# Chunked attention with a cosine feed-forward block: new lists of due times and other matmul lengths in the planner

## The chip, the cores and the metric

The kernel runs on one core of one Trainium2 chip. The metric is the device time of one execution in microseconds (us), as the median of a few executions. The engines are PE (TensorE, matmuls), ACT (ScalarE), DVE (VectorE), POOL (GpSimd) and SP (SyncE, which issues the transfers). Each runs its own instructions in their order and waits on semaphores for the others.

## What is computed

```
B, H, S, D = 8, 8, 576, 64                     # q, k, v are float32
scores = q_c @ k_c.T / sqrt(D)                 # within chunks of 64 positions
attn   = exp(scores - max) / (sum + 1e-9)
x      = (attn @ v_c), heads side by side      # 4608 tokens x 512
h      = x @ w_in                              # 512 x 2048
out    = (h * cos(h)) @ w_out                  # 2048 x 512
```

The weights come as 64-bit floats, and the result has to be near to the 32-bit one.

## The kernel before, in words

The 4608 tokens are worked on in nine tiles of 512 (`TOK`), t = 0 to 8. A matmul of full precision is made of three: each operand is split into a high part (a cast to fp32r) and a low part (the rest), and high x high, high x low and low x high are added up in PSUM. So a product of 128 rows by 512 columns is three matmuls, and the step "hidden" of one block of 128 features is twelve.

First stage (tiles 0 and 1, and the attention of tile 2). Weights are loaded and decoded: two ACT operations and one on DVE (`split_weight`, lines 564 to 571) give a 32-bit weight, then a high and a low part (`copy_by`, lines 503 and 505; `two_by`, line 509). PE takes turns: twelve matmuls of `hidden` (x by w_in, into one of two banks `h`), then twelve of `project` (g by w_out, into four banks `acc`) for the block three back. Between them ACT and DVE make g = h cos(h) by four steps (`activated`, lines 886 to 889: ACT, DVE, ACT, DVE), and then the parts `g_hi` (ACT or DVE) and `g_lo` (DVE or POOL). The last DVE step of the four (line 889) frees the bank of h for the hidden product two blocks later. Attention of the tiles 0 to 2 (scores in 64x64 matmuls) is fitted in between. POOL, DVE and ACT also make sums of weight blocks (`whole_again`, `sums_of_w`, `high_parts`, `low_parts`), which `keep_sums` stores (line 988).

At the end of this stage come the differences of tile 2 (`halves`, lines 1094 and 1104). They are written to the tiles `pts` and `vt`, which also hold tile 1's results on their way out (`finish`; stores at line 958).

From tile 2 on, hidden products are made by seven products in place of eight on halves of the features and of x (Strassen's scheme as Winograd gives it): `single_pair` for tile 2 and `wide_pair` for two tiles at once (3 and 4, 5 and 6, 7 and 8). Their weights are streamed back from memory (`combo`). The scores and weighted sums of the next tiles come between them.

The order of work is made when the program is built. Each step is entered by `piece(engine, length, run, *after, lag, other, main)`; `other` is a second engine that may do it. `in_order` hands all pieces of a stage to `placed`, a model of five engines: it takes the engine that can begin soonest, and of its pieces that can begin within 0.2 us of that the one with the lowest due time, and notes the start. Then the pieces are written into the program by their starts. A step with two engines goes to the one that took it. The due times come from four lists, one for each stage: `DUE_FIRST` (648 pieces), `DUE_SECOND` (1062, tile 2 and tiles 3 and 4), `DUE_NEXT` (596, tiles 5 and 6) and `DUE_LAST` (463, tiles 7 and 8). The search that found lists (`trials`) is switched off here; it minimised the end and the mean start of the matmuls marked `main`.

What the model holds: a length for each piece, a lag to whoever waits, a charge for POOL and DVE at work together (`PORT`), a change of ACT's tables (`TABLE`), a slower PE after a pause, and, in the first stage alone, a delay of PE's instructions. A step on SP is booked with 0.1 to 1.8 us, a store of a result with 0.1 us and 2.5 us more until it has landed (line 1462). The order of the loads of inputs and weights (`FIRST_LOADS`) is fixed, and they are not moved by the lists.

From the second stage on, all PE work is one chain, so the lists leave its order alone:

```
    def pe(length, run, *after):
        stream[0] = piece(PE, length, run, stream[0], *after, main=True)
        return stream[0]
```

In the first stage, `hidden` and `project` are such a chain, and the attention's PE steps can move against it.

Of the kernel before, what the change touches and what calls it, by code (L numbers as in the profile page):

```python
# [159 lines left out]
)  # L160


DUE_SECOND = (
# [296 lines left out]
def attention_then_cos_ffn(ctx: ExitStack, tc, qT, kT, v, w_in, w_out, out, wide):  # L460
# [759 lines left out]
    def made_by(key, run, *args):  # L1220

        def go():
            made[key] = run(*args)
        return go
# [11 lines left out]
    split = {}  # L1236
# [882 lines left out]
```

## Time and profile before

| | us |
|---|---|
| median of 3 runs (lowest to highest) | 792.94 (792.94 to 793.42) |
| the profiled execution | 792.41 |
| its span, first to last instruction | 790.4 |
| PE busy | 772.8 (98%) |
| DVE busy | 579.6 (73%) |
| ACT busy | 473.4 (60%) |
| POOL busy | 302.8 (38%) |

Matmuls overlap: the profile shows each of them with an end that lies past the start of the next one, so a group is best measured from start to start. A wait stands in square brackets behind the instruction that waited, with the idle time of its engine and what ended it. "issue" stands where the profile shows nothing that was waited for. SPq are the queue instructions by which SP starts transfers.

### The profile page before, as it was taken

The page shows a single profiled execution, that of the slowest core. Times are in us where ns is not written, and L with a number is a line of the kernel's source. Part 1 is how long each engine was busy: PE and PEld are TensorE (multiplying, and loading weights), DVE is VectorE, ACT ScalarE, POOL GpSimd, SP SyncE. Part 2 cuts the span into 40 slices and gives each one's busy share as a digit, 9 for nine tenths or more (in the row PEclk, how much of TensorE's full clock was granted, in tenths as well). Part 3 has the DMA queues.
Part 4 walks back from the last instruction along what each step waited for, and adds up shares of the span by engine and source line. Part 5 has one row for each costly group of instructions (what it writes and reads, how often), then busy time and mean ns, then how long its engine had stood idle before and what let it go on. Part 6 is the DMA issues. An engine that isn't in the chain of part 4 may idle for free.

```text
span 790.4 us, 15213 instructions
## 1 busy us (share of the span) xinstructions
PE 772.8 (98%) x5818; PEld 673.7 (85%) x5818; DVE 579.6 (73%) x913; ACT 473.4 (60%) x872; POOL 302.8 (38%) x240
## 2 busy tenths in 40 slices
PE   7999999999989999999999999999999999999997
PEld 6878888887879988888888888888888888888886
DVE  6988898987887898885786968886896664554421
ACT  6999975454866566645664456454763464555522
POOL 3454476556734382211134842221265621221100
PEclk9999999999999999999999999999999999999999
DMA  9992707566975755845646358647553265543431
GB/s 341 412 417 110 241 15 258 182 232 213 321 250 181 221 191 189 296 164 188 222 141 216 113 181 300 191 149 239 171 203 104 78 214 181 189 164 107 158 109 54
DMA packets 72744, 156.19 MB, mean 198 GB/s; under 512 B 7776, under 2 KB 22624, under 8 KB 72672
## 3 DMA queue, kind: packets, MB, share of 16 engines
q1 hardware_dynamic: 72672, 155.22, 57.6%
q8 instruction: 46, 0.75, 0.4%
q14 instruction: 26, 0.21, 0.1%
HBM read 117.44 MB, written 37.75 MB: 196 GB/s over the span
## 4 chain that ended last, share of the span: by engine, by line
PE 85%; ACT 6%; DMA 4%; DVE 3%; issue 1%; POOL 0%; SPq 0%; ACTq 0%; DVEq 0%; POOLq 0%
PE acc L494 44%; PE h L494 32%; PE a L494 9%; DMA w_in<-in_w_in_dram 2%; DMA qt<-in_qT_dram 1%; ACT half L571 1%; ACT w L569 1%; ACT g L888 0%; ACT g L886 0%; DMA out_dram<-pts 0%; ACT g_hi L505 0%; PE a L1321 0%; ACT e L678 0%; DVE pts L509 0%; DMA out_dram<-vt 0%
## 5 line engine op out<-in xcount | busy, mean ns | idle before, releaser
L494 PE MATMUL acc<-w_out,g_hi 128*128 128x512 f32 x1124 | 336.3, 381 | 0.6 <-ACT pts L505 0.6
L494 PEld LDWEIGHTS acc<-w_out,g_hi 128*128 128x128 f32 x1124 | 210.1, 190 | 30.4 <-ACT pts L505 1.0
L509 POOL TENSOR_TENSOR g_lo<-g,g_hi 128x512 fp32r<-128x512 f32 x78 | 109.8, 1410 | 282.7 <-ACT g_hi L505 178.0
L494 PE MATMUL acc<-w_out,g_lo 128*128 128x512 f32 x562 | 213.1, 379 | 0.0
L494 PE MATMUL h<-x,w_in 128*128 128x512 f32 (+1 forms) x864 | 199.0, 357 | 2.9 <-DVE g L889 2.4
L494 PEld LDWEIGHTS h<-x,w_in 128*128 128x128 f32 x864 | 150.0, 190 | 23.9 <-DVE g L889 3.4
L494 PE MATMUL h<-w_in,w_in 128*128 128x512 f32 (+1 forms) x576 | 136.2, 354 | 0.8 <-DVE w_in L1139 0.7
L494 PEld LDWEIGHTS acc<-w_out,g_lo 128*128 128x128 f32 x562 | 106.5, 190 | 15.1
L494 PEld LDWEIGHTS h<-w_in,w_in 128*128 128x128 f32 x576 | 99.2, 190 | 14.4 <-DVE w_in L1139 2.2
L505 ACT CAST g_hi<-g 128x512 fp32r<-128x512 f32 x98 | 60.3, 618 | 44.7 <-PE acc L494 29.2
L1145 DVE SCALAR_TENSOR_TENSOR g<-g,h 128x512 f32<-128x512 int32 (+1 forms) x40 | 23.0, 576 | 73.7 <-ACT g L1142 73.4
L494 PE MATMUL a<-x,w_in 128*128 128x512 f32 x288 | 70.2, 380 | 0.0
L494 PEld LDWEIGHTS a<-x,w_in 128*128 128x128 f32 x288 | 54.2, 189 | 8.2 <-ACT a L1136 0.7
L509 DVE TENSOR_TENSOR g_lo<-g,g_hi 128x512 fp32r<-128x512 f32 x38 | 35.2, 931 | 26.1 <-ACT g_hi L505 24.6
L1136 ACT COPY h<-h 128x512 f32<-128x512 f32 (+1 forms) x40 | 19.4, 485 | 55.4 <-PE h L494 42.7
L1149 ACT ACTIVATE g<-g 128x512 f32<-128x512 f32 (+1 forms) x72 | 41.9, 582 | 17.1 <-DVE g L1145 16.8
L1149 ACT ACTIVATE w_in<-w_in 128x512 f32<-128x512 f32 x48 | 29.8, 628 | 10.1 <-DVE w_in L1145 10.1
L509 POOL TENSOR_TENSOR e<-e,z 128x512 f32<-128x512 f32 x14 | 17.9, 1290 | 43.4 <-DVE z L763 35.6
L505 ACT CAST g_hi<-w_in 128x512 fp32r<-128x512 f32 x24 | 14.9, 620 | 29.2 <-PE acc L494 26.4
L1142 ACT ACTIVATE g<-h 128x512 int32<-128x512 f32 (+1 forms) x40 | 20.5, 511 | 18.2 <-PE h L494 17.3
L1145 DVE SCALAR_TENSOR_TENSOR w_in<-w_in,w_in 128x512 f32<-128x512 int32 x24 | 28.6, 1190 | 2.4 <-ACT w_in L1142 1.2
L888 ACT ACTIVATE g<-g 128x512 f32<-128x512 f32 x32 | 20.2, 631 | 14.6 <-DVE g L887 14.5
(205 smaller groups left out, 1182.4 us busy)
## 6 DMA issues: line engine op xcount, KB each, us to landing
w_in<-combo SPq DMA_DIRECT2D x112, 512.0 KB, 4.0
combo<-w_in SPq DMA_DIRECT2D x56, 256.0 KB, 3.3
gathered<-w_in SPq DMA_DIRECT2D x48, 256.0 KB, 3.5
qt<-in_qT_dram SPq DMA_DIRECT2D x36, 256.0 KB, 4.8
kt<-in_kT_dram SPq DMA_DIRECT2D x36, 256.0 KB, 5.2
w_in<-in_w_in_dram SPq DMA_DIRECT2D x16, 512.0 KB, 9.4
w_out<-in_w_out_dram SPq DMA_DIRECT2D x16, 512.0 KB, 9.6
w_in<-gathered SPq DMA_DIRECT2D x24, 256.0 KB, 3.0
```

Of the source, the lines that this page charges most:

```text
L494: kept(nc.tensor.matmul(*args, **kw))
L505: kept(nc.scalar.copy(out=out, in_=in_))
L509: kept(eng.tensor_tensor(out, a, b, op=op))
L569: lambda: kept(nc.scalar.activation(w(), upper.bitcast(F32), AF.Prelu, scale=2.0 ** -(MORE // 8), alpha=-(2.0**32))),
L571: lambda: kept(nc.scalar.activation(low, lower, AF.Copy, scale=LOWEST)),
L888: lambda: kept(nc.scalar.activation(g, g, AF.Sin, bias=0.5 * math.pi)),
L1136: kept(nc.scalar.copy(out=out, in_=in_))
L1142: kept(nc.scalar.activation(g.bitcast(I32), h, AF.Identity, bias=0.25, scale=0.5 / math.pi))
L1145: kept(nc.vector.scalar_tensor_tensor(g, g.bitcast(I32), -2.0 * math.pi, h, op0=ALU.mult, op1=ALU.add))
L1149: kept(nc.scalar.activation(g, g, AF.Sin, bias=0.5 * math.pi))
```

## The change

Three of the four lists get other numbers, as many as before: `DUE_FIRST`, `DUE_SECOND` and `DUE_NEXT`. `DUE_LAST` stands in the diff as context and is not changed. The correlation of ranks between old and new list is 0.65, 0.76 and 0.69, so the order is another one throughout. The lengths of PE pieces in the planner become shorter: 0.68 to 0.648 for three matmuls of 512 columns, 2.72 to 2.592 for twelve, 0.35 to 0.336, 0.706 to 0.672 and 1.362 to 1.296. No operation is added, removed or changed; what moves is the order on ACT, DVE, POOL and SP, the engine of steps that have two, and in the first stage the place of the attention's PE steps. The first lines of each list:

```diff
 DUE_FIRST = (
-    19.07, 9.7, 18.15, 19.93, 20.46, 14.17, -7.36, 18.95, 59.8, 25.74, 17.73, 33.29, 23.7, 22.9, 47.19, 12.37,
-    19.85, 0.82, 97.2, -15.62, 1.32, 2.6, 14.1, 35.52, 24.56, 26.31, -1.59, 49.53, 35.88, 33.69, -25.45, 38.61,
...
+    8.4, 47.45, -291.79, -58.6, 42.54, 115.52, 3.71, 510.8, 41.47, 33.14, -55.91, 16.87, 25.16, 147.1, -147.69,
+    16.63, 26.11, 22.2, 162.21, -18.7, 29.26, 38.45, -29.26, -4.08, 7.83, 49.32, 81.95, 10.5, 34.24, 24.93, 14.19,
...
 )
 DUE_SECOND = (
-    5.26, 2.29, 11.01, 13.29, 4.38, 3.21, 5.68, 16.46, -34.46, 25.06, 22.89, 86.91, 25.49, 121.17, 37.24, 22.92,
-    25.11, 17.31, 18.05, 45.53, -55.15, -43.44, -15.1, -40.72, -3.76, -60.06, 31.92, 7.1, 11.2, -34.2, -20,
...
+    -12.85, 2.21, 2.31, 3.75, 7.22, 3.78, 4.82, 4.73, 34.21, 4.92, 3.46, 22.89, 82.26, 18.21, 88.69, 755.07,
+    -15.61, 20.48, 21.88, 57.79, 81.17, 0.65, 2.14, 4.32, 2.53, 3.32, 4.25, 39.9, 6.37, 17.38, 107.92, 9.35,
...
 )
 DUE_NEXT = (
-    -39.57, -31.5, -27.38, -30.94, -35.82, -3.65, -25, -26.04, -8.41, -21.66, 15.69, -26.96, -20.56, -17.77,
-    -17.41, 21.43, 12.15, -12.73, 13.68, 12.16, 8.18, 16.96, -8.11, 20.22, -21.39, -14.9, 17.41, -5.99, -14.23,
...
+    20.68, 0.95, -10.86, 1.45, -3.38, -1.44, -17.55, 24.42, 3.81, -5.59, -57.9, 96.14, 11.4, 22.2, -19.2, 78.23,
+    2.02, -57.15, -68.3, 96.01, -8.58, -2.59, 48.9, 6.14, -34.28, -7.27, -5.72, 12.26, 11.5, 12.86, -5.77, 15.17,
...
 )@@ the planner's lengths @@
-                    PE, 0.68, go, stream if cc else None, split["in", fc], bank_at, *x_done[t][2 * cc : 2 * cc + 2],
+                    PE, 0.648, go, stream if cc else None, split["in", fc], bank_at, *x_done[t][2 * cc : 2 * cc + 2],
...
-                PE, 2.72, made_by(key, hidden, t, fc), stream, split["in", fc], bank_at, *before,
+                PE, 2.592, made_by(key, hidden, t, fc), stream, split["in", fc], bank_at, *before,
...
-                PE, 2.72, made_by(key, project, u), stream, given[u], split["out", fu], *free, *before, pairs=12, main=True
+                PE, 2.592, made_by(key, project, u), stream, given[u], split["out", fu], *free, *before, pairs=12, main=True
...
-            0.68 if half is None else 0.35, lambda: out_part(t, fc, sub, half), low_of.get((t, fc)),
+            0.648 if half is None else 0.336, lambda: out_part(t, fc, sub, half), low_of.get((t, fc)),
...
-            return product_piece(7 * k + j, 0.706, go, *deps)
+            return product_piece(7 * k + j, 0.672, go, *deps)
...
-            return product_piece(n0 + j, 1.362, go, *deps, *(x_lows.get((t, j), ()) if k == 0 else ()))
+            return product_piece(n0 + j, 1.296, go, *deps, *(x_lows.get((t, j), ()) if k == 0 else ()))
```

## Rows read from the trace of the kernel before

**Rows 1.** The span cut into stretches (start:end in us), then its length, the busy us and instruction count of each engine, PE's granted clock, the busy share of the transfer engines and GB/s.

```profile
core 0: us, PE busy (x) PEld busy (x) DVE busy (x) ACT busy (x) POOL busy (x), PEclk, DMA share, GB/s
0.00:20.00 20.00, 14.66 (x294) 12.32 (x296) 12.56 (x23) 12.52 (x37) 6.47 (x11) 1.00 0.92 342
20.00:60.00 40.00, 38.86 (x348) 32.40 (x349) 35.80 (x63) 39.58 (x62) 19.75 (x15) 1.00 1.03 414
60.00:100.00 40.00, 39.44 (x241) 34.04 (x240) 35.71 (x50) 38.98 (x63) 19.07 (x15) 1.00 0.47 166
100.00:180.00 80.00, 80.00 (x605) 69.31 (x604) 70.31 (x115) 48.51 (x90) 50.71 (x50) 1.00 0.52 179
180.00:200.00 20.00, 18.21 (x177) 15.55 (x179) 14.03 (x18) 9.74 (x19) 13.73 (x14) 1.00 0.60 207
200.00:220.00 20.00, 18.95 (x163) 16.74 (x154) 16.89 (x38) 17.49 (x58) 13.17 (x15) 1.00 0.88 304
220.00:240.00 20.00, 18.00 (x220) 15.97 (x219) 15.06 (x33) 10.97 (x29) 6.58 (x5) 0.91 0.71 236
240.00:280.00 40.00, 40.00 (x495) 36.62 (x494) 33.16 (x78) 26.23 (x74) 14.62 (x13) 1.00 0.65 206
280.00:300.00 20.00, 19.70 (x110) 17.21 (x110) 18.95 (x21) 12.10 (x25) 17.89 (x11) 1.00 0.62 200
300.00:460.00 160.00, 160.00 (x1213) 139.53 (x1212) 128.36 (x195) 88.74 (x147) 56.39 (x39) 1.00 0.57 186
460.00:620.00 160.00, 159.97 (x1212) 139.53 (x1212) 123.96 (x190) 88.42 (x144) 56.26 (x39) 1.00 0.58 191
620.00:790.40 170.40, 165.05 (x771) 144.53 (x769) 74.84 (x100) 80.16 (x135) 28.20 (x20) 1.00 0.43 142
```

**Rows 2.** The waits of PE over the span: the tile it was to write, what released it, then us in total, times and the longest.

```profile
PE h L494 <- DVE g L889: 2.4, 3, 1.8
PE a L494 <- issue: 2.0, 1, 2.0
...
PE h L494 <- DVE w_in L1139: 0.7, 2, 0.5
```

**Rows 3.** PE in order of time around its stalls: start, us until the shown end of the last of the group, what, and the idle time before it with its releaser.

```profile
38.02 0.48 PE L494 MATMUL h<-x,w_in 128*128 128x512 f32 x1 [0.27 <-DVE g L889]
...
49.88 0.48 PE L494 MATMUL h<-x,w_in 128*128 128x512 f32 x1 [0.34 <-DVE g L889]
...
56.98 0.66 PE L777 MATMUL a<-ident,e 128*128 128x128 f32 x4 [0.30 <-DVE x L851]
...
83.61 0.70 PE L494 MATMUL acc<-w_out,g_hi 128*128 128x512 f32 x2 [0.56 <-ACT pts L505]
...
184.05 0.59 PE L494 MATMUL acc<-w_out,g_hi 128*128 128x512 f32 x2
184.48 0.38 PE L494 MATMUL acc<-w_out,g_lo 128*128 128x512 f32 x1
186.65 0.70 PE L494 MATMUL h<-x,w_in 128*128 128x512 f32 x2 [1.79 <-DVE g L889]
...
208.62 0.94 PE L494 MATMUL h<-w_in,w_in 128*128 128x256 f32 x6 [0.53 <-DVE w_in L1139]
...
210.69 0.49 PE L494 MATMUL h<-x,w_in 128*128 128x256 f32 x2 [0.48 <-DVE g L1152]
...
233.42 0.26 PE L494 MATMUL a<-kt,qt 64*64 64x64 f32 x1 [2.00 <-issue]
...
289.49 0.71 PE L494 MATMUL h<-w_in,w_in 128*128 128x256 f32 x4 [0.22 <-DVE w_in L1139]
```

**Rows 4.** One step of the chain that ended last, where PE is full: start, us, what.

```profile
117.55 2.59 PE h L494 x12
```

**Rows 5.** One stretch right after the wait by "issue", with the columns of the first group.

```profile
233.40:236.80 3.40, 3.38 (x13) 2.71 (x13) 2.84 (x6) 1.29 (x8) 0.00 (x0) 0.50 0.50 169
```

**Rows 6.** The same chain ahead of the stall at 184 us.

```profile
174.18 2.39 DMA out_dram<-vt
...
176.69 0.12 DVE vt L1094
...
179.38 3.38 DMA out_dram<-pts
...
182.84 0.88 DVE pts L1094
...
185.99 0.61 DVE g L889
```

**Rows 7.** SP in order of time at the same place: start, us that the group took to issue, what and how many.

```profile
171.22 2.18 SPq L988 DMA_DIRECT2D combo<-w_in  x4
...
178.75 1.23 SPq L958 DMA_DIRECT2D out_dram<-pts  x2
...
181.12 2.83 SPq L988 DMA_DIRECT2D combo<-w_in  x4
```

**Rows 8.** A subtraction on DVE at two places, and the one on POOL beside the second, in order of time on their engines.

```profile
168.81 0.69 DVE L509 TENSOR_TENSOR g_lo<-g,g_hi 128x512 fp32r<-128x512 f32 x1
...
78.98 1.66 DVE L509 TENSOR_TENSOR w_in<-w,w_in 128x512 fp32r<-128x512 f32 x1
...
78.65 1.45 POOL L509 TENSOR_TENSOR g_lo<-g,g_hi 128x512 fp32r<-128x512 f32 x1
```

307 rows, old and new, of tables (DUE_FIRST, DUE_NEXT, DUE_SECOND) are left out of this document.

## Prediction

> **What bounds the kernel now.** I read the stretches first: for each part of the span the table gives busy time by engine, and the reader is to look at how far TensorE (PE) falls short of the stretch's length [rows 1]. In the first 20 us it lacks 5.34 us, while inputs arrive. After that it lacks 1.14 + 0.56 us up to 100 us, nothing to 180, 1.79 in 180 to 200, 1.05 in 200 to 220, 2.00 in 220 to 240, nothing to 280, 0.30 to 300, and then 0.03 us in the whole 320 us that follow. The last stretch lacks 5.35 us, which is the end of the program after its last matmul. So the kernel is bound by PE, and PE is full from 300 us on. The second view, PE's waits, names who releases it: the cosine product of VectorE (DVE) that frees a bank of `h` (2.4 us in three waits), a 2.0 us wait for which nothing visible is the cause ("issue"), and a sum on DVE (0.7) [rows 2]. The third, PE in order of time, gives each stall its place [rows 3]: 38.02, 49.88, 56.98, 83.61, 186.65, 208.62, 210.69, 233.42 and 289.49 us, nine in all that matter.
>
> Idle time understates a stall, since a matmul's shown end lies past the next one's start. At 184.48 us the next start is 2.17 us away, where twelve matmuls in 2.59 us [rows 4] give 0.216 each: 1.95 us lost. The two matmuls after it take 0.70 us, where such a pair takes 0.59 in the same rows [rows 3]: 0.11 more. That is 2.06 us for 1.79 of idle, so I add 0.27 us for each stall. One stall has a sequel: after 2.00 us of idle at 231 us, the granted clock is 0.50, the lower of the two levels, for 3.40 us [rows 5], which is 1.70 us of work. The 1.79 us of idle at 185 us had no such sequel: the clock of that stretch is 1.00 [rows 1].
>
> What a perfect order could give back after 20 us is therefore 6.87 (idle) + 9 x 0.27 = 2.43 + 1.70 = 11.0 us. No order of the other engines does better without a gain in the loading stage, whose loads are asked for in a fixed list that stays as it is.
>
> **The change, part by part.** The lengths (0.68 to 0.648 for three matmuls, 2.72 to 2.592 for twelve) are only numbers in the planner; no matmul gets shorter. By themselves they are worth 0 us. They do bring the planner to what the chip does: 2.592 is the 2.59 us of the chain [rows 4]. The old plan thought PE 5% slower than it is, so what it called just in time came late on the chip where the other engines had no slack. That is a reason why a search with the new lengths can see stalls that the old one could not, and it holds where engines beside PE are nearly full.
>
> The three new lists rank ACT, DVE, POOL and SP work anew, and let some pieces change engine. No work is added, so I cost each stall group:
>
> (a) 20 to 100 us, 1.70 us idle + 4 stalls x 0.27 = 2.8 us. Here ScalarE (ACT) is busy 78.56 of 80 us: it, not PE, is the tightest. DVE has 8.5 us free and POOL (GpSimd) 41 us [rows 1]. High parts and bank copies may go to DVE, low parts to POOL, so an order that unloads ACT by a few of its 0.6 us casts exists. I take 1.7 us back. Bounds: all 2.8, or 1.0 lost if one stall of the size of 83.61 (0.56 + 0.27) is added.
>
> (b) 184 us, 2.06 us. The chain of waits here is not one of engine load [rows 6]: DVE stands at the differences of the third token tile (line 1094), whose target tiles are still being read by two output stores, landing 2.39 and 3.38 us after their start, and the cosine product that frees PE's bank is queued on DVE behind them. The second of these stores began at 179.38 because SP, in order, had issued other transfers first: 2.18 us for four stores of weight sums, then stores and loads [rows 7]. The planner books 0.1 us of SP for such a step and 2.5 us to landing, and the new code keeps both numbers. So the search does not see the cause; it can help only by moving the differences or the cosine product. I take 0.6 us back, less than a third. Bounds: all 2.06, or the loss of rival 3.
>
> (c) 200 to 220 and 280 to 300 us, 1.35 us idle + 3 x 0.27 = 2.2 us. These wait for a sum and a cosine product of single pairs [rows 2, 3], chains of short steps between PE products whose order is fixed by the program. I take 0.6 back; bounds 2.2, or 0.5 lost (one such stall more).
>
> (d) 231 us, 2.00 + 0.27 + 1.70 = 4.0 us. PE stands in the middle of 128 short score matmuls and waits for nothing that the profile shows. I take it for the delivery of its own instructions (that nothing else shows is my only ground), and PE's order in this stage is a chain fixed by the program, with the same count before it. The second list does not steer it. I take 0 back; bounds 0 and 4.0, the latter if the number of waits inserted ahead of it shifts the point.
>
> (e) After 300 us, 0.03 us idle. Two lists (the second's later half and the third) reorder stages which cannot get better. I take 0.3 us lost, one small stall; bounds 0 and 1.6 (two stalls like 208.62, 0.53 + 0.27 each).
>
> Sum: -1.7 - 0.6 - 0.6 - 0 + 0.3 = -2.6 us. The profiled execution took 792.41 us (span 790.4 and 2.0 around it), so 789.8 on its terms; the runs shown have a median 0.53 us higher, so 792.94 - 2.6 = **790.3 us**.
>
> **Where a page speaks against it.** A subtraction on DVE (`g_lo` and the weights' low parts, line 509) took 0.69 us at 168.81 us with POOL idle, and 1.66 us at 78.98 us, while POOL ran one of the same kind from 78.65 on [rows 8]. So work sent to POOL in stretch (a) is not free: at up to 0.97 us each, nine more pieces on POOL use up DVE's 8.5 us, and then nothing of (a) comes back. The Trainium skill (GPSIMD Engine Reference, 1. Specifications) says that GpSimd's interfaces to SBUF are shared with VectorE and contend with VectorE instructions that have two SBUF inputs; both operations are of that kind, and the trace agrees. By that rule taken alone the sum would be -2.6 + 1.7 = -0.9 us. The planner has a term for this, so I leave (a) as it is and give the case to rival 2.
>
> **Rivals.** 1. The stall at 231 us goes too, or shrinks to nothing: -2.6 - 4.0 gives 786.3 us. For it: its place hangs on a count of instructions, and waits are inserted anew by the new order. Against it: the matmuls ahead of it are the same in number. 13%.
>
> 2. The order changes and the time does not. The stalls at 184 and 231 us, 6.1 of the 11.0 us, have causes that the planner does not hold (SP's issue time, instruction delivery), and (a) is held back by POOL's contention; what comes back is lost in (e). Time 792.9 us, within 1.6 either way. 26%.
>
> 3. Slower: the wait on the output stores grows. At 181.12 us SP issues four more stores of weight sums, 2.83 us [rows 7]. If the new order makes these sums ready before the last output stores, SP issues them first, the store that DVE waits for lands 2.83 us later, and PE's idle of 1.79 becomes 4.6. It decides from 2.00 us of idle on, where the clock fell at 231 us: then 1.70 us come on top. +2.83 + 1.70, the 0.6 of (b) not gained, the rest as forecast (-1.7 - 0.6 + 0.3): +2.5, so 795.4 us. For it: neither SP's time nor the order of its issues is in the plan. Against it: the sums wait for POOL, which was busy 13.73 of 20 us there. 18%.
>
> **How the numbers follow.** The forecast has 43%, rival 1 13%, rival 2 26%, rival 3 18%. A change of under 0.2% (1.6 us) can't be told from none. Faster is forecast and rival 1, 0.56; same 0.26; slower 0.18. The likeliest case's own range is 787.5 to 791.3: from half of what it could still gain in (a) to (c), to the edge of what can be told. The range of all goes from 785.0, where (a) to (c) come back whole (7.1 us) and a little of (d), to 795.4, rival 3.
>
> **What would show it right or wrong.** Right: the stalls at 38 to 84 us mostly gone, with ACT's busy share in 20 to 100 us a little lower; a stall near 180 us still released by a DVE product behind line 1094 and an output store; a stall of about 2 us by "issue" among the score matmuls with half the clock after it; and 0.3 us or less of idle after 300 us. Wrong: the early stalls unchanged, a clock that fell at a second place, or new idle after 300 us. If the loading stage's 5.34 us of idle shrinks, I missed a source of gain, since I hold it bound by loads that stay as they are.

## The result: 0.6% slower, and the profile after

The changed kernel took 797.13 us (median of 6, 796.36 to 797.84), the kernel before on the same chip 792.94 (median of 6, 791.88 to 795.56): a ratio of 1.006 with a 95% interval of 1.0045 to 1.0076. The forecast was 790.3 us with a range up to 795.4, so the time lies outside it, on the other side. The profiled execution of the changed kernel took 796.36 us (span 794.6), 4.0 us more than that of before (792.41, span 790.4).

All line numbers of the changed kernel are higher by one: its line 495 is the matmul of line 494, 890 the product of 889, 1095 the difference of 1094. First its span in stretches, with the columns of [rows 1]:

```profile
0.00:20.00 20.00, 15.11 (x260) 12.91 (x260) 11.21 (x23) 11.26 (x34) 5.73 (x10) 1.00 0.93 343
20.00:60.00 40.00, 38.33 (x376) 32.26 (x377) 36.28 (x63) 38.77 (x62) 22.47 (x18) 1.00 1.03 414
60.00:100.00 40.00, 40.00 (x245) 34.85 (x244) 34.09 (x48) 38.67 (x61) 23.59 (x18) 1.00 0.48 166
100.00:180.00 80.00, 78.14 (x594) 67.32 (x593) 66.47 (x102) 47.39 (x85) 49.10 (x51) 1.00 0.49 171
180.00:200.00 20.00, 17.55 (x81) 14.74 (x80) 17.57 (x22) 10.66 (x22) 13.71 (x11) 1.00 0.60 193
200.00:220.00 20.00, 18.92 (x239) 16.71 (x238) 16.68 (x32) 16.55 (x53) 13.85 (x15) 1.00 0.92 310
220.00:240.00 20.00, 19.28 (x239) 17.27 (x238) 17.64 (x40) 15.19 (x41) 7.11 (x7) 1.00 0.82 267
280.00:300.00 20.00, 18.94 (x108) 16.88 (x108) 17.65 (x19) 12.52 (x25) 16.91 (x11) 1.00 0.61 188
300.00:460.00 160.00, 159.34 (x1208) 138.56 (x1207) 122.99 (x194) 89.17 (x147) 56.98 (x39) 1.00 0.57 188
460.00:620.00 160.00, 158.30 (x1201) 137.09 (x1200) 122.13 (x191) 86.81 (x143) 49.56 (x35) 1.00 0.58 191
```

Compare PE's busy time with the length of each stretch, and with [rows 1]. PE was full from 100 to 180 us and short by 0.03 us from 300 to 620; now it lacks 1.86 us in the first, and 0.66 + 1.70 = 2.36 us in the second. Past 20 us, two stretches are better. 60 to 100 us is full (0.56 us short before), but 20 to 60 us lost as much (1.67 for 1.14). 220 to 240 us is 0.72 us short (2.00 before), and the granted clock is 1.00 where it was 0.91.

The new stalls, PE in order of time as in [rows 3]:

```profile
128.86 1.16 PE L495 MATMUL a<-kt,qt 64*64 64x64 f32 x64 [1.50 <-issue]
183.52 0.70 PE L495 MATMUL h<-x,w_in 128*128 128x512 f32 x2 [1.51 <-DVE g L890]
189.90 1.35 PE L495 MATMUL h<-x,w_in 128*128 128x512 f32 x5 [0.93 <-DVE g L890]
495.64 1.56 PE L495 MATMUL h<-w_in,w_in 128*128 128x512 f32 x6 [0.62 <-ACT h L1137]
585.10 0.48 PE L495 MATMUL acc<-w_out,g_lo 128*128 128x512 f32 x1 [0.98 <-POOL g_lo L510]
```

I measured every stall over 0.3 us in both traces from matmul start to matmul start, as the forecast did for the one at 184 us, and added them up by stretch. Left out is a gap of 0.40 us at 20.02 us in the kernel before, the end of the loading. The stall at 231 us has its 1.70 us of half clock [rows 5] with it:

| us | before | after | difference |
|---|---|---|---|
| 20 to 100 | 2.13 | 2.07 | -0.06 |
| 100 to 180 | 0 | 2.19 | +2.19 |
| 180 to 200 | 1.95 | 2.78 | +0.83 |
| 200 to 230, without the next | 1.33 | 2.45 | +1.12 |
| stall at 231, with half clock | 3.90 | 0 | -3.90 |
| 280 to 300 | 0.38 | 1.22 | +0.84 |
| 300 to 460 | 0 | 1.18 | +1.18 |
| 460 to 620 | 0 | 2.19 | +2.19 |
| sum | 9.69 | 14.08 | +4.39 |

The span grew by 4.2 us. Against the sum stand 0.45 us less idle in the first 20 us (4.89 after, 5.34 before) and the 0.40 us at 20.02 us; 0.7 us I can't place. So the lists cost about 8.3 us in stalls, and 3.9 us came back at a place where the forecast expected nothing.

Three views name what the new stalls wait for. DVE and SP around 182 us (start, us, what; idle before it and its releaser):

```profile
182.17 0.69 DVE L1095 TENSOR_TENSOR pts<-e 128x512 f32<-128x512 f32 x1 [6.52 <-DMA out_dram<-pts]
182.78 0.68 DVE L890 TENSOR_TENSOR g<-h,g 128x512 f32<-128x512 f32 x1
```

```profile
174.85 2.20 SPq L989 DMA_DIRECT2D combo<-w_in  x4
177.14 1.97 SPq L959 DMA_DIRECT2D out_dram<-pts  x3
```

DVE stands 6.52 us at the difference that overwrites `pts`, and the product that frees PE's bank is queued behind it. The store that it waits for left SP after four stores of weight sums, which took 2.20 us. In the wide stages it is ACT that stands. Its waits for these transfers over the span, in the changed kernel; the kernel before had one of 1.0 us and one of 2.8 us:

```profile
ACT w_in L1143 <- DMA gathered<-w_in: 11.5, 5, 3.8
ACT g_hi L506 <- DMA w_in<-gathered: 6.6, 3, 2.7
```

The last of them, ACT and SP in order of time:

```profile
580.76 0.63 ACT L1143 ACTIVATE w_in<-w_in 128x512 int32<-128x512 f32 x1 [3.76 <-DMA gathered<-w_in]
...
582.75 1.27 ACT L506 CAST g_hi<-g 128x512 fp32r<-128x512 f32 x2
```

```profile
572.99 2.91 SPq L492 DMA_DIRECT2D w_in<-combo  x2
576.01 0.37 SPq L1757 DMA_DIRECT2D gathered<-w_in  x1
```

ACT may not overwrite `w_in` before its store to `gathered` has left it. That store stood on SP behind two loads. ACT's casts of `g_hi` came after it, then POOL's `g_lo`, for which PE waited 0.98 us.

### The profile page after: what moved, and what is told of

It is laid out like the page before. It is cut to its first block, busy times and chain, and to the rows that moved or that the text cites. A ratio compares the mean times of both kernels' runs of the same rounds, so it can differ in the third digit from the quotient of the medians.

```text
span 794.6 us, 15217 instructions
## 1 busy us (share of the span) xinstructions
PE 773.1 (97%) x5818; PEld 673.4 (85%) x5818; DVE 573.5 (72%) x908; ACT 474.2 (60%) x874; POOL 307.5 (39%) x243
## 4 chain that ended last, share of the span: by engine, by line
PE 82%; ACT 5%; DVE 4%; DMA 4%; issue 2%; SPq 1%; POOL 1%; ACTq 0%; DVEq 0%; POOLq 0%
PE acc L495 42%; PE h L495 31%; PE a L495 9%; DMA w_in<-in_w_in_dram 2%; DMA kt<-in_kT_dram 1%; ACT w L570 1%; ACT half L572 1%; SPq L492 1%; DMA gathered<-w_in 1%; DVE w L565 1%; DMA out_dram<-pts 1%; ACT g L889 0%; ACT L889 0%; ACT g L887 0%; DVE g L888 0%
## 5 line engine op out<-in xcount | busy, mean ns | idle before, releaser
L510 POOL TENSOR_TENSOR g_lo<-g,g_hi 128x512 fp32r<-128x512 f32 x75 | 107.9, 1440 | 271.7 <-ACT g_hi L506 124.3
L1140 DVE TENSOR_TENSOR w_in<-h,w_in 128x512 f32<-128x512 f32 (+1 forms) x40 | 22.6, 582 | 15.4 <-PE h L495 10.6
L1153 DVE TENSOR_TENSOR g<-w_in,g 128x512 f32<-128x512 f32 x32 | 28.5, 892 | 3.7 <-ACT g L1150 2.8
L565 DVE SCALAR_TENSOR_TENSOR w<-w,half 128x512 uint32<-128x512 uint32 x32 | 27.6, 866 | 3.9 <-ACT w L570 2.7
```

The lines of the kernel that those rows point to most:

```text
L510: kept(eng.tensor_tensor(out, a, b, op=op))
L565: kept(nc.vector.scalar_tensor_tensor(bits, bits, 3, low, op0=ALU.logical_shift_left, op1=ALU.bitwise_or))
L1140: kept(nc.vector.tensor_tensor(out, a, b, op=ALU.add))
L1153: kept(nc.vector.tensor_tensor(g, h, g, op=ALU.mult))
```

## Experiments

**One list at a time.** Both sets of lists and lengths stand in one program, and a flag for each of the four stages chooses the set; each stage keeps exactly the order that its parent has there (the state that the planner hands from stage to stage is set to the parent's). The edit, shown at two of its places:

```diff
+NEW = (1, 0, 0, 0)
...
-                PE, 2.592, made_by(key, hidden, t, fc), stream, split["in", fc], bank_at, *before,
+                PE, 2.592 if NEW[0] else 2.72, made_by(key, hidden, t, fc), stream, split["in", fc], bank_at, *before,
...
-        close(ends, DUE_SECOND if u == 1 else DUE_NEXT)
+        close(ends, ((OLD_SECOND, DUE_SECOND) if u == 1 else (OLD_NEXT, DUE_NEXT))[NEW[now[0]]])
```

First stage alone, flags (1, 0, 0, 0):

> First stage planned with the new list and new lengths, the three later stages in the order of the kernel before. From the starts of the same score matmuls in the two traces (198.50 against 201.75 us) the first stage lost 3.25 us. Theory (each list brings its own stalls, and the stall at 231 us is a delivery of instructions held up behind loads that the second list places): the first stage's loss comes alone and the stall near 233 us with its half clock is there again, so 792.9 + 3.2 = 796.2 us. Rival (the stall at 231 us hangs on the count of PE instructions in the first stage): it is gone here, so 796.2 - 4.2 = 792.0.

791.15 us, ratio 0.9975 (0.9961 to 0.9990). Four stalls of the changed kernel's first stage are there, each within 0.3 us (0.98 at 53 us, 1.66 at 126, 1.40 at 181, 1.10 at 188). The first score matmul after 229 us starts 2.4 us later than before, at 231.73. And the stall at 231 us with its half clock is gone. So the first list costs 2.4 us and takes away a stall that belongs to the second stage; the time is near the rival's 792.0 us and far from the theory's 796.2.

Second stage alone, (0, 1, 0, 0):

> Second stage alone by the new list and lengths. Between the same matmuls the second stage gained 1.4 us net: 4.2 for the stall at 231 us with its half clock, less 2.8 of new stalls. Theory: 792.9 - 1.4 = 791.5 us, no half clock. Rival (count of instructions in the first stage): the stall stays, 792.9 + 2.8 = 795.7 us.

791.87 us, ratio 0.997 (0.9957 to 0.9983). The stall at 231 us is 0.33 us. The second list's own are there: 0.65, 0.88, 1.21, 0.40, 0.37 and 0.45 us at 215, 222, 290, 311, 368 and 388 us. The time is the theory's; but as the first list alone takes the stall at 231 us away too, neither list is its one cause.

Third alone, (0, 0, 1, 0):

> Third list (tiles 5 and 6) alone, with its lengths. The starts of the same matmuls say +2.3 us for this stage, which was free of stalls before. Theory: 792.9 + 2.3 = 795.2 us, with stalls of some 0.8 and 1.4 us near 493 and 580 us, each behind an ACT step that waits for a store of the kept g. Rival (the stage loses only because the stage ahead of it left other work over): 792.9 us, no stall after 460 us.

794.83 us, ratio 1.0014 (0.9999 to 1.0029). It loses 1.96 us at 493 us, and 0.47 and 1.14 us at 583. The stall at 231 us (2.54 us) and its half clock stay.

Fourth alone, (0, 0, 0, 1), where the list is the old one and only lengths differ:

> Last stage alone, whose list is the same and whose lengths in the planner are the new ones. The traces show no stall there in either kernel. Theory: 792.9 us within 0.5. Rival (the shorter lengths themselves take away slack that the chip needs): 0.5 us or more above.

792.25 us, ratio 0.998 (0.9967 to 0.9993), with no new stall after 235 us (the 0.38 us at 290 us is that of the kernel before). The new lengths do no harm there. Why the time is 1.0 us below the kernel before the trace doesn't say.

All but the third, (1, 1, 0, 1):

> The changed kernel with the old list and old lengths in the stage of the tiles 5 and 6 alone. Theory (each stage's loss is its own): the stalls at 493 to 584 us go, 2.3 us: 794.8 us. Rival (a stage's loss is made up or passed on by the next): within 1 us of the changed kernel's 797.1.

793.27 us, ratio 1.0001 (0.9991 to 1.0012), 3.9 us under the changed kernel's median where 2.3 were expected. Its PE is full from 460 to 620 us, so the third list's loss is its own and nothing makes it up later. The theory stands, its size was low: this stage has 2.19 us of stalls in the profile, and the third list alone cost 1.6 us, so not all of the 3.9 us is explained. Nor do the first and the second list add up: each alone was 1.4 to 2.1 us under the kernel before, since each takes away the same stall at 231 us, and together (with the last stage's lengths) they gain nothing.

The new lengths with all the old lists:

> The new lengths with the old lists. A due time is only a rank within the run of the planner's model. Theory (lists and lengths belong together: with other lengths the same ranks give another order with more stalls): over 800 us. Rival (ranks carry over): 793 us within 2.

One execution: 822.25 us, with PE short in every stretch (153.73 of 160 us busy in 300 to 460). These lists belong to the lengths they came with; the last stage's list did not suffer from the new ones (run e4).

**Who issues the stores.** Tile 1's results leave through `pts` and `vt`. In the first of these runs they leave by other tiles (`w` and `half`), on top of the extra matmuls of run e5 further down:

```diff
-        if t == 1 or not whole:
+        if not whole:
```

> The same as the run before, and tile 1's results leave through the tiles of the weight sums (w, half) in place of vt and pts, so that the differences of tile 2 on DVE share no tile with an output store. Theory (the 2.06 us stall at 184 us is DVE's wait for those stores): it goes, 788.7 - 2.0 = 786.7 us. Rival (the cosine product would come late anyway, or the sums on POOL now wait for the stores and hold the start of the second stage): 788.7 us or more.

799.26 us, ratio 1.0079 (1.0052 to 1.0106). The theory fell as I had put it. DVE in order of time:

```profile
188.55 0.69 DVE L509 TENSOR_TENSOR w<-w_in 128x512 f32<-128x512 f32 x1 [8.33 <-DMA out_dram<-w]
```

Another room moves the wait to whoever uses that room next, here the weight sums. DVE waits 8.33 us for a store that SP issued only at 183.31 us; in the kernel before it had waited 3.05 us for the store of `pts`. What stays is the rival: the store leaves late. So the next edits leave the tiles alone and let POOL issue the stores: the products h cos(h) that a wide stage sets aside for the second of its two tiles (`gathered`) in the kernel of run e3, tile 1's results in the changed kernel and in the kernel before, and both in the changed kernel.

```diff
-                kept(nc.sync.dma_start(out=gathered[fc], in_=v[g]))
+                kept(nc.gpsimd.dma_start(out=gathered[fc], in_=v[g]))
...
-            nc.sync.dma_start(out=to, in_=os[b::2])
+            (nc.gpsimd if t == 1 else nc.sync).dma_start(out=to, in_=os[b::2])
```

> The third list alone, as before, but with the stores of the kept g issued by POOL instead of SP (in all three wide stages), so that they do not stand behind loads on SP. Theory (the new stalls of this stage, 1.96 us at 493 and 1.6 us at 583, come from ACT waiting for such a store that SP issued late): both go, and the run is 2.5 us or more below that with the third list alone, at some 792.3 us. Rival (ACT and POOL are late there by their own work): the stalls stay, 794.8 us or more, POOL's issuing added.

793.37 us, ratio 1.0002 (0.9982 to 1.0022): the stalls at 493 and 583 us are gone (0.31 us at 587 stays). So the third list's stalls are the wait for SP. The time agrees, but less sharply: 0.7 us above the kernel before in place of 1.6, with intervals that overlap.

> The changed kernel with tile 1's results alone issued by GpSimd in place of SP. Theory: DVE's wait of 6.52 us for the store of `pts` falls to under 3, the stall at 181.6 us (1.68) goes: 795.4 us; the stalls at 494.6 and 583 us stay. Rival (the store's own 4.22 us bounds it, whoever issues it): 797.

795.08 us, ratio to the kernel before 1.0033 (1.0018 to 1.0047). DVE's wait for the store is 3.27 us in place of 6.52 (the store lands 2.07 us earlier, and DVE comes to it 1.18 us later), the stall at 182 us is gone, and the rest is untouched:

```profile
180.10 0.70 DVE L1095 TENSOR_TENSOR pts<-e 128x512 f32<-128x512 f32 x1 [3.27 <-DMA out_dram<-pts]
```

> The changed kernel with two kinds of stores issued by GpSimd in place of SP: tile 1's results (the store in `finish`) and the rounded weights of the wide stages (`gathered`). Order otherwise as changed. Theory (SP issues in order, so a store that is ready waits behind others; the planner books SP 0.1 us): the stall at 181.6 us (1.68) goes or falls under 0.5, those at 494.6 (0.78) and 583 (1.41) go, about 3.5 us together: 793.6 us. Rival (the stores are late by the transfer itself, or GpSimd issues them later than SP would because it works in order too): 797 or more.

792.90 us, ratio 0.9995 (0.9976 to 1.0014): 4.2 us under the changed kernel, with no stall left at 182 or 494 us and 0.22 us at 592. ACT's wait of 3.76 us at 581 us is now:

```profile
579.34 0.63 ACT L1143 ACTIVATE w_in<-w_in 128x512 int32<-128x512 f32 x1 [1.73 <-DMA gathered<-w_in]
```

Two edits on who issues the stores give back all that the change had lost, without touching a list.

> The kernel before with tile 1's results issued by GpSimd in place of SP. Theory: the second store of `pts` starts when its copy is made and not at 179.38 us, the stall at 184.5 us (2.06 us) goes: 2 us faster, 790.7 us, the stall at 231 us with its half clock unchanged. Rival: GpSimd is 13.7 of 20 us busy there and issues late, or the transfer bounds it: 792.7 us, within 1.

790.42 us, ratio 0.997 (0.9957 to 0.9983). The stall at 184 us fell from 1.95 to 1.21 us, not to nothing:

```profile
186.86 2.86 PE L494 MATMUL h<-x,w_in 128*128 128x512 f32 x12 [1.05 <-DVE g L889]
```

The one at 231 us stayed (2.00), but in the profiled execution no half clock followed. So the time is as the theory had it, but by another sum: 0.74 us of that stall and, in this execution, 1.70 of half clock. Over all runs the second part is an estimate: a mean granted clock of 0.9986 against 0.9972 for the kernel before beside it is worth 0.0014 x 790 = 1.1 us.

**What the stall at 231 us is.** The queue that brings instructions, in a short stretch: packets, MB and share. Of the kernel before from 230.8 to 231.2 us, just before PE stands:

```profile
q8 instruction: 1, 0.02, 14.7%
```

Of the changed kernel from 231.4 to 231.6 us, 2 us before its score matmuls, which start at 233.43 us:

```profile
q8 instruction: 1, 0.02, 27.5%
```

Each kernel has 46 such packets in all (0.75 MB, so 16 KB each). In the kernel before, the first of the 128 score matmuls starts at 229.31 us and the packet is fetched 1.56 us later; PE runs out of instructions and goes on at 233.42 us, 1.61 us after this packet has ended. In the changed kernel it comes before the score matmuls. The Trainium skill (Runtime: NRT & Kernel Launch, The ~15µs preamble/postamble breakdown) says that instructions are fetched ahead without an instruction asking for it; the trace agrees, as nothing issues these packets. That one fetched late stalls PE is shown by the runs here.

Counting PE's own instructions (matmuls, weight loads, semaphores) in the traces makes the place plain. In all 19 traces, the n-th packet, from 0, never begins before PE has begun 256n + 152 of them (874 packets). In all nine traces that have the stall at 231 us, PE stops with 4033 begun, whatever the order of the other engines. So the packet after number 3736 (n = 14) has the time of 297 instructions, many of them short, to come. In the kernel before it began 5.7 us after that number and was too late; in the changed kernel it began 2.3 us after it. What delays a packet is not settled. In the traces the median delay is 0.9 us where other transfers moved under 50 GB/s in the following us, and 3.2 us where they moved over 330; no run changed that alone.

To move the fetches I put 24 products of 64x64 (48 matmuls and as many weight loads in the trace, where the expectation counts 48 instructions) into an idle run of PE at 10.4 us of the plan:

```diff
+        for _ in range(small):
+            matmul(b[:CH, :CH], ident[:CH, :CH], ident[:CH, :CH], start=True, stop=True)
...
+    fills += [piece(PE, 0.135 * 8, lambda: idle_run(8, 24), *fills[:1], at=10.4, pairs=8) for i in range(FILLS)]
```

> The kernel before with 24 small matmuls (64x64) more in the idle run at 10.4 us, which lie in a wait of PE and write a bank that is read by nobody. They move every later point of PE's program by 48 instructions against the blocks in which the instructions are fetched. In the kernel before the fetch began 1.56 us after the start of the score matmuls at 229.31 us; where it began before them (first list or second list alone) the stall was 0.3 us or less. Theory (the stall comes where a fetch meets the start of the 128 short matmuls): the fetch comes earlier, no stall near 231 us, no half clock, 792.9 - 4.2 = 788.7 us. Rival (the fetch is held up by the loads issued at 224 to 226 us, whatever its place): stall and half clock stay, 793 us.

791.43 us, ratio 0.9978 (0.9954 to 1.0002), span 788.0. The stall at 231 us is gone with its half clock, and no list was touched. The start takes 2.3 us longer, and the stall at 184 us is 1.20 us for 1.95, though SP issues the stores as before; so that stall does not depend on the issuer alone. The interval reaches to no change. The edit also moves the fetch away from the loads that SP issues from 224 us on, so it doesn't tell the count of instructions from those loads as the reason why the fetch came late.

A second execution of each kernel:

> The kernel before once more, for a second profile of the same program. If the instruction fetch among the score matmuls at 231 us falls at the same place in each execution, it starts 1.56 us after the first of them again, with 2.2 us lost and the half clock after it. If its time varies by executions, the start and the half clock differ: in runs of the same order up to there it began 1.2 to 2.1 us after the first one and cost 1.7 to 2.5 us.

> The changed kernel once more, for a second profile of the same program. Theory: the stalls made by order (127, 182, 189, 224, 292, 495 and 583 us) come again within 0.3 us each, and none at 231 us, since the fetch began 2.0 us ahead of the score matmuls. Rival (fetches vary by 2 us): a stall among them.

The kernel before took 790.52 us this time. PE in order of time, and the stretch of [rows 5]:

```profile
232.91 0.21 PE L494 MATMUL a<-kt,qt 64*64 64x64 f32 x1 [1.28 <-issue]
```

```profile
233.40:236.80 3.40, 3.40 (x23) 3.13 (x23) 3.34 (x8) 1.33 (x9) 0.00 (x0) 1.00 0.62 211
```

The same program now waited 1.28 us in place of 2.00, and its clock stayed at 1.00. All other stalls before 230 us came back within 0.1 us. So of the 3.9 us in my table, 0.7 of the stall and the whole half clock belong to that execution and not to the kernel. Over the 133 executions of the kernel before in these comparisons the mean granted clock goes with the time: a median of 792.04 us for the 60 with 0.998 or more, 795.69 us for the 22 with 0.995 or less. One stretch of 3.4 us at half clock lowers the mean by 0.002 alone, so the lowest ones lost some elsewhere; where, these runs don't show. The changed kernel took 796.14 us, with its stalls again at the same places, each within 0.3 us, and none at 231 us.

**Putting gains together.** Second list, new lengths in the last stage, and tile 1's stores by POOL:

> Old first and third list with their old lengths, the new second list and the new lengths in the second and the last stage, and tile 1's results issued by GpSimd. Theory (gains and losses belong to places and add up): relative to the kernel before -1.3 (new second list, with the stall at 231 us gone), -1.0 (last stage), -2 to -2.4 (stores): 788.4 us, half of the stall at 184 us left, none at 231 us. Rival (the stores' gain in the run on the old order was the half clock at 231 us, which the new second list takes away already): 790.5 us.

792.18 us, ratio 0.9977 (0.9961 to 0.9994), above both expectations. The order of the second stage is that of run e2, whose stall at 231 us was 0.33 us; here:

```profile
233.50 0.21 PE L674 MATMUL a<-kt,qt 64*64 64x64 f32 x1 [1.77 <-issue]
```

Its score matmuls start 1.42 us earlier (229.63 us for 231.05), mostly as the stall at 184 us is 0.86 us for 1.98, and the fetch does not come earlier with them (231.11 us for 230.85). What was saved ahead of the fetch was lost in it.

The extra matmuls of e5 and tile 1's stores by POOL:

> The kernel before, with tile 1's results issued by GpSimd and 24 matmuls of 64x64 more in each idle run at 10.4 us (the place of PE's instruction fetches moves). Theory: the stall at 231 us goes (2.0), the one at 184 us is halved (0.85), 1.6 us more at the start as in the run with the matmuls alone: 790.0 us. Rival as in the other run: the stores' gain was the half clock, and the two together give no more than the 24 matmuls alone, 791.4 us.

790.68 us, ratio 0.9967 (0.9948 to 0.9985), between the two expectations; no stall at 231 us, 0.53 at 184 us, and a new one of 1.19 us at 203, after a fetch at 201.71 us.

The stores by POOL with the new lengths in the last stage:

> The kernel before in its first three stages, the new lengths in the last one, and tile 1's results issued by GpSimd. Theory (what was measured for each adds up): -1.0 and -2.4 relative to the kernel before, 790.4 us where that takes 793.75. Rival (the last stage's -1.0 was within its interval's reach of the noise): as the stores alone, 791.4 us.

792.78 us, ratio 0.9995 (0.998 to 1.0009): above both expectations. Up to 231 us its order is that of e11; its stall at 184 us is 0.86 us, but at 231 us it lost 1.92 us, and half the clock followed for 3.4 us. So gains smaller than what that fetch varies by do not add up. Runs e11 and e14 have the lowest medians here, both under the kernel before with an interval that leaves out 1. Run e2 has the same ratio as e11 (0.997), and which of these is the fastest can't be told.

## Why the prediction was wrong

The step that failed is the price of a new order. The forecast booked gains of 2.9 us at the old stalls, (a) to (c), and almost no loss where PE was full: nothing for 100 to 180 us and 0.3 us after 300 us. Measured were 2.7 us lost in place of the gains, 2.19 us lost in 100 to 180 us and 3.4 us after 300 us. The 3.9 us that came back at 231 us were aimed at by nothing in the change and are in part luck of the execution profiled before.

**(a), 20 to 100 us, forecast -1.7.** Failed. ACT was relieved as I had thought possible (77.44 us busy of 80, before 78.56), and POOL took more (46.06 us, before 38.82). The stalls stayed the same size all the same: 2.07 us for 2.13. That an order exists which unloads ACT was right; that the stalls then go was shown by no row. The worse error is next to it: 100 to 180 us, full before, has no term in the sum, and it lost 2.19 us. The profile names no releaser for the 1.66 us at 127 us ("issue"). By the times it is DVE:

```profile
120.21 3.52 DVE L510 TENSOR_TENSOR w_in<-half,w_in 128x256 fp32r<-128x256 f32 x4
...
127.47 1.28 DVE L714 TENSOR_TENSOR e<-a,m 128x512 f32<-128x512 f32 x2
```

Four subtractions took 3.52 us, DVE then stood 0.74 us for ACT, and the softmax step that reads the scores ended at 128.75 us, 0.11 us before PE went on. That order on DVE is read from the trace; it was not tested. A smaller slip: 0.23 us of the 1.14 us of idle between 20 and 60 us lie at 20.02 us, in none of the four stalls of (a).

**(b), 184 us, forecast -0.6.** The mechanism was right and the sign wrong. SP's time is in the plan with far less than it takes, so the search couldn't see the cause, as I wrote; I still booked a gain. The planner books 0.1 us of SP for the four stores of weight sums (line 1480 of the kernel before), which took 2.20 us, and 2.5 us until a result has landed (line 1433, not 1462), where the store took 4.22. Measured: +0.83 us, one stall by the store (1.68) and one of DVE's order (1.10). Runs e9, e10 and e11 show that the wait for SP's issue can be taken away; e11 also shows that some of the stall is left when it is, and e5 that the stall shrinks as much with the stores left on SP.

**(c), 200 to 230 and 280 to 300 us, forecast -0.6.** +1.12 and +0.84 us, against a bound of 0.5. Run e2 has them with the old first list, so they are the second list's. What they wait for is read from the trace and not tested. At 218 and 225 us ACT had just loaded a table (1.28 us each time). At 293 us the product that PE waits for stood on DVE behind two subtractions that took over twice the 0.69 us of [rows 8], while POOL ran subtractions too:

```profile
288.94 1.78 DVE L510 TENSOR_TENSOR x<-vt,x 128x512 fp32r<-128x512 f32 x1
...
290.97 1.44 DVE L510 TENSOR_TENSOR vt<-w_in,w_in 128x512 f32<-128x512 f32 x1
```

**(d), 231 us, forecast 0.** That it is the delivery of instructions was right: e5 and the packets show it. The sentence "The second list does not steer it", drawn from PE's fixed order and the same count before it, was the error. The count does fix the place: PE stops at the same instruction in all nine traces with the stall. It does not fix whether, and for how long: e2 and e13 have the same count, and one lost 0.33 us, the other 1.98. That hangs on when PE gets there and on how late the packet comes, which alone made the cost 1.5 us in e16 and 2.5 us in e3, two of five traces with the same order up to there. What delays the packet stays open. It gave back 3.9 us in the two profiles compared; from 1.5 to 3.9 in the two of before. I had the bound (4.0) and rival 1, which had it right for this one place: it says that the place hangs on a count of instructions.

**(e), after 300 us, forecast +0.3 with a bound of 1.6.** Measured +3.4 (1.18 + 2.19). A stage that is full can only lose, and I sized the loss by two stalls of the kind that I had seen, on DVE. The larger part, 2.19 us, was a transfer queued on SP (e7, e9), of which [rows 7] showed the kind but at another place. The planner books nothing on SP for the loads of `combo` there, as they are issued inside a step of PE (line 1133 of the kernel before); two of them took 2.91 us.

**The lengths, forecast 0.** Not so by themselves: with the old lists they cost 29.6 us in the one execution of e8 (822.25 us for 792.66). That no matmul gets shorter was right, but a due time is a rank within the planner's run, and with other lengths the same ranks give another order.

**The rivals.** Rival 3 named the cause that mattered, stores issued late by SP, and its time of 795.4 us was 1.7 us low; but it put it into one place, with a fall of the clock that didn't come, and gave it 18%. Its condition for that fall, 2.00 us of idle, held up no better: the clock fell after 1.72 us in e15 and not after 1.80 in e11. The late stores were in truth at 182, 494 and 583 us. Rival 2 (no change) saw that what the plan does not hold can't be found, and not that it can be made worse. Of the likeliest case's own range, the lower end does not come out as described: half of what (a) to (c) could still gain, 7.1 - 2.9, is 2.1 us and gives 788.2 us, not 787.5. By the rule of the Trainium skill (GPSIMD Engine Reference, 1. Specifications) that the forecast weighed at +1.7 us, nothing would have come back in (a), and nothing did. That POOL was the reason is not shown.

The chances came out wrong since I read the lists as a chance to remove stalls. The kernel before had 0.03 us of idle in 320 us: its old order fitted waits that the planner books too short or not at all. A new order drawn by the same planner need not keep that, and this one didn't.

## What to carry to other kernels

Where a planner books too little for a resource (here SP's issues and the landing of stores), an order made anew can lose wherever that resource is in use, also in stages that were full: bound the loss over the whole span, and not at the stalls that exist. Before a stall by "issue" is costed, profile the same program a second time; one that varies can hide or fake a gain of its own size. When one instruction waits for a store, look at who stands ahead of that store on its queue: here two kinds of stores, issued by another engine, were worth as much (4.2 us) as the whole change cost.

## What the runs showed of the hardware

- A fetch of instructions (16 KB) that began 1.05 to 2.09 us after the start of 128 short score matmuls cost PE 1.5 to 2.5 us. The packets come one for 256 of PE's instructions, none before instruction 256n + 152, and PE stopped at the same instruction each time.
- The granted clock fell to half for about 3.4 us after some of those stalls (idle 2.34 us in e3, 2.10 in e4, 2.00 in the kernel before, 1.72 in e15) and stayed at 1.00 after others (1.80 in e11, 1.77 in e13, 1.52 in e7, 1.28 in e16). So the length of the stall alone does not decide it.
- A transfer issued by POOL took POOL about 0.55 us (1.63 us for three). Two additions of weight blocks on DVE took 1.29 us together in the changed kernel, and 3.34 in e10, while POOL issued stores and then ran a subtraction:

```profile
172.90 3.34 DVE L510 TENSOR_TENSOR w<-w_in 128x512 f32<-128x512 f32 x2
```

```profile
174.39 1.28 POOL L510 TENSOR_TENSOR g_lo<-g,g_hi 128x512 fp32r<-128x512 f32 x1
175.61 1.63 POOL L959 DMA_DIRECT2D out_dram<-pts  x3
```

What of this is the issue of stores and what the subtraction, no run here separates.
